# Attention stage of a four-layer kernel: the last pair of residual rows is loaded two steps later in the order, unused query columns hold ones, and whole output tiles are written

## The chip, the cores and the metric

The kernel runs on one core of a Trainium2 chip. The metric is the device time in microseconds (us); the median of the runs counts. The engines are PE (matrix multiply, with its weight load PEld), DVE (vector), ACT (scalar, activation functions), POOL (GpSimd) and SP, which here only issues DMAs. Each engine works through its own list of instructions in order; a DMA waits in its engine's list until its operands are ready, and what stands behind it in that list waits too.

## The reference

Four layers A, B, A, B with residuals, x of shape 1 x 2048 x 576:

```python
x = x + _A_ref(_layernorm(x), A_wqkv, A_wo)
x = x + _B_ref(_layernorm(x), B_w_in, B_w_sp, B_b_sp, B_w_out)
x = x + _A_ref(_layernorm(x), A_wqkv, A_wo)
x = x + _B_ref(_layernorm(x), B_w_in, B_w_sp, B_b_sp, B_w_out)
```

A is attention with 32 heads of 18 columns, in which each position looks at 8 keys: itself and the positions 2, 4, ... 14 before it. B is a gated layer: `z = gelu(x @ w_in)`, its second half is layer-normed and mixed over the sequence by a 2048 x 2048 matrix plus a bias, multiplied with the first half, and projected back by `w_out`.

## The kernel before

**Tiles of layer A.** The sequence is cut into 18 query tiles t of 114 rows (`QT`; tiles 8 and 17 have 112). A tile's keys are its own rows and the 14 before them, so 128 partitions of keys. Each tile is worked in two halves of 16 heads: steps s = 2t and 2t+1, 36 steps in all. In step s, PE computes the logits of step s+1 (`L_mm`, line 445), ACT takes the exponential into `P_sb` (`EXP`, line 454), PE multiplies the probabilities of step s with the values (`PV`, line 465; `v_ext` has a column of ones per head, so the sum of the probabilities comes out as a 19th column), and DVE divides: a reciprocal of those sums (`rec`, line 471) and a multiplication (line 472) into `o_t`. `P_sb` has 128 query columns, of which only 114 are computed; `setup_bufs` (lines 367 to 372) clears the others once, and clears the unused rows and columns of the three `o_t` buffers.

**From o_t to the residual.** After the second half of tile t, SP issues a DMA that transposes `o_t` into `o_slot` (line 475; called "transpose t" below). DVE copies the result into a ring `oT` (`O_CP`, line 484). The last two tiles are transposed on PE instead (`O_T`, line 490). When the ring holds 128 complete rows, PE projects row tile i with the output weights in two halves of the columns (`WO(i, 0)` and `WO(i, 1)`, line 510), and DVE adds the old x (`xo`) to give `x_new` (line 513). Then follow the statistics of the layer norm (DVE, lines 220 to 224, POOL line 225), the normalized rows (`LN_XN`, POOL lines 245 and 248, 2.3 us and 0.24 us), the store of `x_new` (`XST`, SP) and the transpose of the normalized rows into `xnT` for layer B (`LN_T`, SP, line 252). In layer 0 the normalized rows 4 to 12 are put into old staging buffers (`stg`).

**Residual loads.** `XO(i)` loads the old x of rows i and i+1 for even i in one DMA on SP, into one of two buffers `xo`. The buffer of pair 14 is that of pair 10, so the load must wait until `WO(11, 1)` has been added.

**Order.** All five engines follow one hand-made table: `at(s, f)` puts f into step s, after `PV(s)`, in the order in which `at` was called. With `row_step` as it is, both attention layers have `WO(11, 0)` in step 31, `WO(11, 1)` and `WO(12, 0)` in step 32, `WO(13, 0)` in step 34 and `WO(14, 0)` in step 35. `XO` is put five steps ahead of `WO`, so `XO(14)` stands in step 30 and `XO(12)` in step 27. Transpose 15 is issued by `PV(31)`, and its copy `O_CP(15)` stands in step 33.

**Layer B** follows without a break: in its first phase PE computes z (line 815), ACT applies gelu (line 829, into one of three buffers `zp`) and squares (line 833), DVE squares the rest (line 831) and normalizes (line 856), and POOL normalizes one block (line 858). POOL first issues the load of the bias (`b_sp`) into the memory that held the normalized rows of layer A; it waits until the last `LN_T` has read them. Then come phases in which PE is busy throughout (lines 905, 929, 971).

Of the kernel before, what the change touches and what calls it, by code (L numbers as in the profile page):

```python
# [10 lines left out]
ALU = mybir.AluOpType  # L11
# [7 lines left out]
P = 128  # L19
D = 576  # L20
H = 32
DH = 18
# [3 lines left out]
QT = P - HALO  # L26
# [39 lines left out]
class K:  # L66
# [258 lines left out]
    def layer_A(self, li):  # L325
        nc, tc, cfg = self.nc, self.tc, self.cfg
# [32 lines left out]
        def tdim(t):  # L359
            nq = cfg.tiles[t][1]  # L360
            return HALO + nq, nq
# [4 lines left out]

        def setup_bufs(eng):
            for pb in P_bufs:
                eng.memset(pb[:, :, :, QT:P], 0.0)
            for ob_ in o_bufs:  # L370
                eng.memset(ob_[96:P, :], 0.0)
                eng.memset(ob_[0:96, D:640], 0.0)

        def exp_table():
            nc.scalar.activation(out=P_bufs[0][:, 0, 0, 0:1], in_=self.ones[:, 0:1], func=ACT.Exp)
# [81 lines left out]
        def PV(s):  # L457
            t, hf = divmod(s, 2)
            nk, nq = tdim(t)
            O_ps = self.PT_tile([P, 512], f32, "O_ps")  # L460
            for jp in range(2):
                for ftl in range(4):
                    for jj in range(2):
                        idx = 4 * ftl + 2 * jp + jj
                        nc.tensor.matmul(O_ps[:, idx * (DH + 1):(idx + 1) * (DH + 1)],  # L465
                                         lhsT=P_bufs[(2 * s + jp) % 4][:nk, jj, ftl, :],
                                         rhs=v_ext[:nk, t, 16 * hf + idx, :], start=True, stop=True)
            Ov = O_ps[:, 0:16 * (DH + 1)].rearrange("p (h e) -> p h e", e=DH + 1)
            o_t = o_bufs[t % len(o_bufs)]
            rec = sb.tile([P, 16], f32, name="rec", tag="rec", bufs=2)  # L470
            nc.vector.reciprocal(out=rec[:nq, :], in_=Ov[:nq, :, DH])
            nc.vector.tensor_tensor(out=o_t[:nq, 288 * hf:288 * (hf + 1)].rearrange("p (h d) -> p h d", d=DH),
                                    in0=Ov[:nq, :, 0:DH], in1=rec[:nq, :, None].to_broadcast([nq, 16, DH]), op=ALU.mult)
            if hf == 1 and t < NT - 2:
                nc.sync.dma_start_transpose(out=o_slots[t % NSLOT][:], in_=o_t[:, :])

# [58 lines left out]
        if li == 0:  # L535
# [74 lines left out]
            R_(2, 2)  # L610
            rows[1]()
            setup_bufs(nc.gpsimd)
            rows[2](nc.gpsimd)
            A_(2, 3)
# [36 lines left out]
        else:  # L651
            for k_, (d, cc) in enumerate([(d, cc) for d in range(5) for cc in range(2)]):
                for qk in ((1, 0) if d < 4 else (0,)):
                    PG(d, qk, cc, k_ == 0, (nc.gpsimd, nc.sync, nc.gpsimd))
                if k_ == 0:
                    setup_bufs(nc.vector)
                    nc.vector.memset(v_ext[:, :, :, DH:DH + 1], 1.0)
                    self.fill_window_rows(QK, 0)
                    exp_table()
                if k_ == 1:  # L660
                    self.run_deferred()
                if k_ == 6:
                    self.fill_window_rows(QK, 1)
# [15 lines left out]
        def at(s, f, *a):  # L679
            table.setdefault(s, []).append((f, a))  # L680
# [12 lines left out]
        row_step = {}  # L693
# [5 lines left out]
                at(2 * t + (5 if li == 0 and t < 10 else 4), O_CP, t)  # L699
        for i in range(NS):  # L700
            s = row_step[i]
            at(s - 5, XO, i)
            at(s, WO, i, 0)
            at(s + 1, WO, i, 1)
            at(s + 1, LN_STATS, i)
            at(s + 2, LN_XN, i)
            at(s + 2, XST, i)
            if i < NS - 1:
                at(max(s + 4, 24 + (5 * i) // 4) if li == 0 else s + 4, LN_T, i)
# [21 lines left out]
        for s in range(NST):  # L731
            if s + 1 < NST:
                L_mm(s + 1)
                EXP(s + 1)
            PV(s)
            for f, a in table.pop(s, []):
                f(*a)
# [345 lines left out]
```

## Time and profile before

| | us |
|---|---|
| runs, median (lowest to highest of 3) | 1190.45 (1189.31 to 1191.66) |
| profiled execution, its own time | 1192.44 |
| span in its profile | 1190.6 |
| PE busy | 1167.5 (98%) |
| DVE busy | 554.3 (47%) |
| ACT busy | 376.9 (32%) |
| POOL busy | 285.9 (24%) |
| mean granted PE clock | 0.997 |

The profiled execution takes 1.84 us more than its span, and 1.99 us more than the median of the runs. In the profile "issue" is time in which an engine waited for nothing that is shown, SPq is SP's list of DMA issues, and `[0.5 <-X]` behind an instruction says that its engine stood idle 0.5 us before it and what ended that. Layer 0 (attention) lies at about 0 to 132 us, layer 1 at 132 to 598, layer 2 (attention) at 598 to 723, layer 3 at 723 to the end.

### The profile page before, as it was taken

What the parts mean: (1) busy time and instruction counts of PE and PEld (TensorE: products, weight loads), DVE (VectorE), ACT (ScalarE), POOL (GpSimd) and SP (SyncE); (2) the same over time, 40 slices, a digit from 0 to 9 for tenths busy, and PEclk for the clock granted to TensorE, in tenths of its full rate; (3) what the DMA queues carried; (4) which work ended last, traced back from release to release, by engine and by line L of the source; (5) the groups of instructions that cost most, each with busy time, mean ns of one, the idle gap of its engine ahead of it and who ended that gap; (6) DMA issues with size and microseconds to landing.
All of it is one profiled execution on the core that took longest, in us unless ns stands there. A gap on an engine that the chain in (4) does not pass through costs nothing.

```text
span 1190.6 us, 20417 instructions
## 1 busy us (share of the span) xinstructions
PE 1167.5 (98%) x8307; PEld 623.4 (52%) x8406; DVE 554.3 (47%) x1235; ACT 376.9 (32%) x621; POOL 285.9 (24%) x386
## 2 busy tenths in 40 slices
PE   9999999999999999999999989999999999999998
PEld 5567544444444444457755765444444444444676
DVE  8788676323233233235456875863223233232321
ACT  5578677111110111102156875770111110111000
POOL 4768774000000000002153876840000000000000
PEclk9999999999999999999999998999999999999999
DMA  7999993000000000059656997900000000001332
GB/s 190 200 173 203 188 220 58 23 12 12 12 1 12 12 12 1 18 169 275 159 94 128 207 211 168 231 10 14 12 12 12 12 1 12 12 1 35 117 105 73
DMA packets 179478, 101.57 MB, mean 85 GB/s; under 512 B 135711, under 2 KB 160735, under 8 KB 179384
## 3 DMA queue, kind: packets, MB, share of 16 engines
q1 hardware_dynamic: 166520, 78.50, 30.6%
q0 software_dynamic: 6512, 16.00, 5.4%
q10 hardware_dynamic: 6352, 5.75, 1.6%
q8 instruction: 66, 1.08, 0.4%
q14 instruction: 28, 0.23, 0.1%
HBM read 42.39 MB, written 16.53 MB: 49 GB/s over the span
## 4 chain that ended last, share of the span: by engine, by line
PE 89%; DMA 3%; POOL 3%; DVE 2%; issue 1%; ACT 1%; SPq 0%; ACTq 0%; POOLq 0%; DVEq 0%
PE pg L929 42%; PE po L971 12%; PE pz L815 10%; PE pz L905 6%; PE pz1s L905 6%; PE pp L410 4%; PE pw L510 2%; PE O_ps L465 2%; PE pv L387 2%; PE L_ps L445 2%; DMA o_slot<-o_t 2%; PE pzs L815 2%; POOL QK L80 1%; DMA xnT<-ln_xn 1%; ACT P_sb L454 1%
## 5 line engine op out<-in xcount | busy, mean ns | idle before, releaser
L929 PE MATMUL pg<-Wq,Z 128*128 128x512 bf16 x2258 | 497.8, 379 | 2.5
L929 PEld LDWEIGHTS <-Z 128*128 128x128 bf16 x2304 | 225.4, 98 | 271.8
L933 DVE TENSOR_TENSOR g_tmp<-pg,ln_xn 128x512 f32<-128x512 f32 x144 | 99.5, 691 | 422.3 <-PE pg L929 422.3
L924 ACT ACTIVATE z1T<-pz 128x1024 bf16<-128x1024 f32 x36 | 34.9, 1020 | 497.4 <-PE pz L905 493.8
L80 POOL DMA_DIRECT2D wout<-in_B_w_out_dram x4 | 4.3, 1064 | 600.8 <-PE pg L929 600.8
L971 PE MATMUL po<-wout,Z 128*128 128x288 bf16 x1152 | 141.4, 286 | 0.0
L454 ACT ACTIVATE P_sb<-L_ps 128x912 bf16<-128x912 f32 (+1 forms) x144 | 125.8, 929 | 39.9 <-PE L_ps L445 39.1
L971 PEld LDWEIGHTS <-Z 128*128 128x128 bf16 x1152 | 112.7, 98 | 28.8
L815 PEld LDWEIGHTS <-xnT 128*128 128x128 bf16 (+1 forms) x800 | 66.5, 97 | 83.7 <-issue 26.5
L815 PE MATMUL pz<-win2a,xnT 128*128 128x512 bf16 x380 | 103.9, 380 | 2.4 <-ACT zp L829 1.6
L934 DVE TENSOR_TENSOR Z<-g_tmp,z1T 128x512 bf16<-128x512 f32 x144 | 99.7, 692 | 12.9 <-DVE g_tmp L933 0.9
L905 PEld LDWEIGHTS <-w 128*128 128x128 bf16 (+1 forms) x640 | 53.7, 97 | 74.0 <-issue 13.6
L410 PE MATMUL pp<-xnT,wqk_sb 128*128 128x512 bf16 x341 | 81.4, 379 | 2.2 <-DMA xnT<-ln_xn 0.9
L829 ACT ACTIVATE zp<-pz 128x1024 bf16<-128x1024 f32 x64 | 65.4, 1022 | 35.4 <-PE pz L815 16.9
L981 DVE TENSOR_TENSOR x_new<-po,xo 128x288 f32<-128x288 f32 (+1 forms) x64 | 28.8, 455 | 87.8 <-PE po L971 84.3
L905 PE MATMUL pz<-xnT,w 128*128 128x512 bf16 (+1 forms) x314 | 66.2, 380 | 0.3
L905 PE MATMUL pz1s<-xnT,w 128*128 128x512 bf16 (+1 forms) x312 | 65.3, 379 | 0.7 <-issue 0.6
L831 DVE CUSTOM_DVE_ANT_0 Z<-zp 128x1536 bf16<-128x1536 bf16 x32 | 56.5, 1765 | 15.6 <-ACT zp L829 10.0
L815 PE MATMUL pz<-win2b,xnT 64*128 64x512 bf16 (+1 forms) x240 | 59.7, 380 | 0.0
L80 POOL DMA_DIRECT2D QK<-stg x81 | 50.6, 630 | 36.7 <-DVE stg L379 18.5
L245 POOL TENSOR_SCALAR ln_xn<-x_new,ln_mv,ln_rstd 128x576 bf16<-128x576 f32 x23 | 54.4, 2367 | 2.0
L510 PE MATMUL pw<-wo_sb,oT 128*128 128x288 bf16 x320 | 50.7, 296 | 3.8 <-DVE oT L484 3.7
(120 smaller groups left out, 1008.3 us busy)
## 6 DMA issues: line engine op xcount, KB each, us to landing
xres<-x_new SPq DMA_DIRECT2D x48, 288.0 KB
xo<-xres SPq DMA_DIRECT2D x32, 288.0 KB
wout<-in_B_w_out_dram POOLq DMA_DIRECT2D x4, 1296.0 KB, 8.3
xo<-xres SPq DMA_DIRECT2D x8, 576.0 KB
w<-in_B_w_in_dram SPq DMA_DIRECT2D x16, 256.0 KB
QK<-stg POOLq DMA_DIRECT2D x53, 72.0 KB, 4.6
QK<-stg SPq DMA_DIRECT2D x41, 72.0 KB
xo<-in_A_x_dram SPq DMA_DIRECT2D x8, 288.0 KB
```

What stands on the lines that cost most here:

```text
L80: return eng.dma_start(out=out, in_=in_)
L410: nc.tensor.matmul(pp[:, :], lhsT=w, rhs=self.xnT[:, c, PADL + cc * 512:PADL + (cc + 1) * 512], start=(c == 0), stop=(c == 4))
L454: nc.scalar.activation(out=P_bufs[(2 * s + jp) % 4][:nk, :, :, 0:nq], in_=Lv[:nk, :, :, 0:nq], func=ACT.Exp, scale=scale)
L510: nc.tensor.matmul(pw[:, 0:288], lhsT=oT[:, c, r0:r0 + P], rhs=wo_sb[:, c, hh * 288:(hh + 1) * 288], start=(c == 0), stop=(c == 4))
L815: nc.tensor.matmul(pzvs[ci][:, sub * 512:sub * 512 + w], lhsT=self.xnT[r0:r1, c, PADL + i * P:PADL + (i + 1) * P], rhs=win2(c)[r0:r1, c0 + ...
L829: nc.scalar.activation(out=zp[:, c0:c0 + cn], in_=pzvs[ci][:, 0:cn], func=ACT.Gelu_apprx_tanh, accum_out=sums[:, ci:ci + 1])
L831: nc.vector.tensor_tensor_reduce(out=spare[:, 0:SQ_D], in0=zp[:, 0:SQ_D], in1=zp[:, 0:SQ_D], scale=1.0, scalar=0.0, op0=ALU.mult, op1=ALU. ...
L905: nc.tensor.matmul(outs[a_], lhsT=w1[r0:r1, c, sub * P:(sub + 1) * P], rhs=self.xnT[r0:r1, c, PADL + q * 512:PADL + (q + 1) * 512], start= ...
L929: nc.tensor.matmul(pg[:, :], lhsT=Z[:, jj, i, sub * P:(sub + 1) * P], rhs=Wq[q][:, i, :], start=(i == 0), stop=(i == NS - 1))
L933: nc.vector.tensor_tensor(out=tmp[:], in0=pg[:, :], in1=bsp[:, qs], op=ALU.add)
L934: nc.vector.tensor_tensor(out=uT(jj)[:, sub, qs], in0=tmp[:], in1=z1Ts[jj, sub][:, qs], op=ALU.mult)
L971: nc.tensor.matmul(acc[hh], lhsT=uT(j // 2)[:, j % 2, i * P:(i + 1) * P], rhs=wouts[j // NJH][:, j % NJH, hh * 288:(hh + 1) * 288], start= ...
```

## The change

```diff
         def setup_bufs(eng):
             for pb in P_bufs:
-                eng.memset(pb[:, :, :, QT:P], 0.0)
+                eng.memset(pb[:, :, :, QT:P], 1.0)
             for ob_ in o_bufs:
-                eng.memset(ob_[96:P, :], 0.0)
-                eng.memset(ob_[0:96, D:640], 0.0)
+                eng.memset(ob_[:, D:640], 0.0)
...
-            nc.vector.reciprocal(out=rec[:nq, :], in_=Ov[:nq, :, DH])
-            nc.vector.tensor_tensor(out=o_t[:nq, 288 * hf:288 * (hf + 1)].rearrange("p (h d) -> p h d", d=DH),
-                                    in0=Ov[:nq, :, 0:DH], in1=rec[:nq, :, None].to_broadcast([nq, 16, DH]), op=ALU.mult)
+            nc.vector.reciprocal(out=rec[:], in_=Ov[:, :, DH])
+            nc.vector.tensor_tensor(out=o_t[:, 288 * hf:288 * (hf + 1)].rearrange("p (h d) -> p h d", d=DH),
+                                    in0=Ov[:, :, 0:DH], in1=rec[:, :, None].to_broadcast([P, 16, DH]), op=ALU.mult)
...
         for i in range(NS):
             s = row_step[i]
-            at(s - 5, XO, i)
+            if i % 2 == 0:
+                at(max(s - 5, row_step[i - 3] + 1) if i >= 4 else s - 5, XO, i)
             at(s, WO, i, 0)
             at(s + 1, WO, i, 1)
```

With ones in the unused query columns, the sums of the unused output rows are positive numbers, so that all 128 rows can be divided and written, and `o_t` needs clearing only in columns 576 to 639. `setup_bufs` runs on POOL in layer 0 and on DVE in layer 2; in both its six `o_t` memsets (three of 32 x 640 and three of 96 x 64) become three of 128 x 64, and its four `P_sb` memsets stay. In layer 2 these four wrote 128 x 56 words of 32 bits each before and write 128 x 112 bf16 values now. Lines from 372 to 700 move up by one number.

`XO` for odd i did nothing before, so leaving it out changes nothing. `XO(12)` goes from step 27 to 28, with no other SP instruction between. `XO(14)` goes from step 30 to 32. The lists of SP's instructions differ in this one place per attention layer. In layer 0 the order was XO(14), transpose 15, LN_T, XST(10), LN_T; it is now transpose 15, LN_T, XST(10), LN_T, XO(14). In layer 2 it was XO(14), transpose 15, LN_T(9), XST(10); it is now transpose 15, LN_T(9), XST(10), XO(14). PE's and ACT's lists keep their order, DVE's and POOL's lose the three memsets each. PE's `O_T` no longer waits for POOL's clearing.

## The prediction

> **What bounds the kernel now.** I read the engines' shares on the page first, then the chain of waits, then the timelines at the two ends of attention.
>
> ```profile
> PE 1167.5 (98%) x8307; PEld 623.4 (52%) x8406; DVE 554.3 (47%) x1235; ACT 376.9 (32%) x621; POOL 285.9 (24%) x386
> ```
>
> PE is busy 98% and holds 89% of the chain, so a change off PE can only win PE's few gaps, or matmuls that ran at a lower clock. The largest gap that touches the edited code lies at the end of layer 2. The chain there:
>
> ```profile
> 708.31 0.02 SPq L80
> 708.33 0.05 issue
> 708.38 5.78 DMA o_slot<-o_t
> 714.16 0.02 issue
> 714.18 0.35 DVE oT L484
> 714.53 0.05 issue
> 714.58 1.38 PE pw L510 x5
> ```
>
> PE waits for O_CP(15), that for transpose 15, and that for an SP instruction of line 80. SP's timeline says which:
>
> ```profile
> 703.26 0.57 SPq L80 DMA_DIRECT2D xres<-x_new  x1
> 707.96 0.37 SPq L80 DMA_DIRECT2D xo<-xres  x1
> 708.38 1.20 SPq L475 DMA_TRANSPOSE o_slot<-o_t  x1
> ```
>
> SP stands from 703.83 to 707.96 at XO(14), whose buffer is still read. The DVE and PE rows show who has waited for what:
>
> ```profile
> 705.00 0.46 DVE L472 TENSOR_TENSOR o_t<-O_ps,rec 114x288 bf16<-114x288 f32 x1
> 707.49 0.45 DVE L513 TENSOR_TENSOR x_new<-pw,xo 128x288 f32<-128x288 f32 x1
> 711.67 0.15 DVE L224 TENSOR_SCALAR ln_rstd<-ln_mv 128x1 f32<-128x1 f32 x1
> 714.18 0.34 DVE L484 COPY oT<-o_slot 128x570 bf16<-128x570 bf16 x1 [2.36 <-DMA o_slot<-o_t]
> 714.58 1.38 PE L510 MATMUL pw<-wo_sb,oT 128*128 128x288 bf16 x5 [3.04 <-DVE oT L484]
> ```
>
> Tile 15 was complete at 705.46; WO(11, 1) freed the xo buffer at 707.94. DVE had nothing to do from 711.82 to 714.18, PE from 711.54 to 714.58. The gap costs twice, as three stretches of 1 us show (first the stretch and its length, then each engine's busy time; the third number from the right is PE's granted clock, 1.00 in full):
>
> ```profile
> 714.00:715.00 1.00, 0.42 (x2) 0.28 (x3) 0.78 (x3) 0.00 (x0) 1.00 (x1) 0.50 1.07 352
> 719.00:720.00 1.00, 1.00 (x6) 0.60 (x4) 0.86 (x4) 0.00 (x0) 0.14 (x1) 0.50 0.60 235
> 721.00:722.00 1.00, 0.93 (x7) 0.49 (x6) 0.89 (x3) 0.98 (x2) 1.00 (x1) 1.00 0.20 76
> ```
>
> The clock is 1.00 up to 713, falls in the microsecond from there, and is 0.50 until about 720.5. Layer 0 runs the same instructions at full clock: there the same group of five starts at 126.52 after 0.62 us idle, and the last WO ends at 132.17, 5.65 us later. Layer 2 needs 714.58 to 722.93, 8.35 us. So the low clock costs 2.7 us.
>
> **Part 1, XO(14) in layer 2.** Transpose 15 can be issued at about 705.5 in place of 708.38. It took 5.78 us behind the 576 KB load; transpose 14 took 5.23. Landing at 710.7 to 711.3 is ahead of 711.82, when DVE comes to O_CP(15), so DVE's own list is late next: 2.36 us are won and 0.68 of PE's 3.04 us remain, like layer 0's 0.62, which kept the clock. PE's end of attention is then 712.22 + 5.65 = 717.87, 5.05 us earlier. Not all of that lasts. POOL's chain of normalized rows is next: it starts row 13 at 719.87 before; in layer 0 it starts 3.90 us after PE's group of five (130.42 against 126.52), so at 716.12 now, 3.75 us earlier. At about 3.2 us a row it then runs back to back to row 15, whose LN_T frees the memory for the bias load; behind that load stands the first normalized block (line 858), which frees the first zp. Before, ACT already waited for that, 1.29 us at 738.89, and PE's fifth row began at 740.06 with no room left. So PE gives back 1.3 us near 736, and 3.7 us remain. Bounds: 2.4 (DVE's wait alone, clock or POOL give nothing) and 5.05 (POOL is not late).
>
> **What the moved load costs.** XO(14) issues behind LN_T(9) (rows ready since 703.34), and XST(10). Their issue takes 1.2, 1.3 and 0.6 us: XO(14) at about 708.75, 0.8 later than before. Row 14 needs it at 719.73 before, at 716.0 now (layer 0: 3.77 after the group of five). Cover 7.2 us; transpose 15, issued right behind it and waiting in the same list, landed 6.2 us after XO(14) was issued. I cost it at nothing; without cover every us late is a us of DVE's addition.
>
> **Part 2, XO(14) in layer 0.** SP was free at 121.25 and issued XO(14) at 121.87; tile 15's rows had been there since 119.37. SP then issues without a pause until 137.67, ending with LN_T(12) and XST(15), and these end the wait of ACT's line 833 at 139.74, after which PE has 1.58 us idle at 141.73. SP's list is what is late, so its stall less one issue gap (0.62 - 0.1), 0.5 us, is won; bounds 0.3 (DVE's wait at O_CP(15) alone) and 0.7. XO(14) itself now issues behind transpose 15, two LN_T and XST(10) at 126.0, and row 14's addition comes at 130.29 - 0.3. Four us of cover against 3.83 for transpose 15 here and 5.78 in layer 2: up to 1.8 us late. That is hidden by POOL, which starts row 14 at 133.63, 1.3 us after its statistics: I cost it at 0, with 0.5 as the bad end.
>
> **Part 3, setup.** In layer 0 POOL's list holds up DVE:
>
> ```profile
> 11.87 0.63 POOL L371 MEMSET o_t<- 32x640 bf16 x1
> 12.54 0.15 POOL L372 MEMSET o_t<- 96x64 bf16 x1
> 15.26 0.73 POOL L576 TENSOR_TENSOR lnx_rstd<-lnx_rstd,neg_half 128x2 f32<-128x2 f32 x1
> 16.03 0.77 DVE L583 TENSOR_SCALAR ln_xn<-x_in,lnx_mv,lnx_rstd 128x576 bf16<-128x576 bf16 x2 [2.27 <-POOL lnx_rstd L576]
> 23.31 10.95 PE L410 MATMUL pp<-xnT,wqk_sb 128*128 128x512 bf16 x49 [0.40 <-DMA xnT<-ln_xn]
> ```
>
> Six memsets take 11.87 to 14.46; three of 128 x 64 at 0.15 take 0.45, so POOL and DVE win 2.1 us. PE is busy from 12.89 to 22.91 with other work and waits only 0.40 us for these rows, then 0.52 at 52.12 for later ones. I take 0.6; bounds 0 (transfers fill the time: their share is about 1 up to 16 us and again from 44) and 0.92. In layer 2 the six take 1.6 us of DVE's time, but DVE then stands idle 1.96 us ahead of 605.25 for another reason: 0. The four P_sb memsets in their new form cost at most POOL's 0.19 us each for the same size, against 0.105: 0.34 us, inside the same idle time.
>
> **Part 4, 128 rows instead of 114.** 72 reciprocals and 72 multiplications. The rows of 112 and 114 partitions take 0.24, 0.25 and 0.46, 0.46; the addition on 128 x 288 takes 0.45. Partitions cost nothing; 0. If time grew with them (12% of 0.71 us, 72 times) DVE would lose 6.1 us, partly beside PE; the rows exclude it. PE's PV already writes all 128 rows, so nothing is added there.
>
> **Sum.** 3.7 + 0.5 + 0.6 = 4.8 us. The profiled execution of 1192.44 (span 1190.6 and 1.84 around it) would become 1187.6; the median of the runs is 1.99 lower and becomes 1190.45 - 4.8 = 1185.65, say 1185.6.
>
> **A rule against it.** The row: PE last worked at 711.54 before the gap, and the clock fell between 713 and 714. The Trainium skill, "TensorE: Matmul & The Clock Gate", Part 1, has the clock halve after an idle window of about 3.4 us that runs freely; by that page a gap of 3.04 us need not halve it in every run, and the sum would then be 3.5 us, the first rival. The trace has it after a shorter gap, so I take the trace.
>
> **Rivals.** *The clock is not won:* it stays low after 712, or the unprofiled runs of before did not lose it. For it: a gap of 0.68 remains behind one of 0.42. Against: layer 0 has 0.41 and 0.62 at clock 1.00. Layer 2 then gives 2.4, the sum 3.5: 1187.0. *The transpose does not land earlier:* it is issued earlier but queues behind LN_T(8) and XST(9), so layer 2 gives nothing. For: transfers at a share above 1 from 695 to 705. Against: the share is 0.00 at 707 to 708, the queue has run dry. Then 1.1 remain: 1189.4. *Slower, the late residual load:* XO(14) takes longer in its new place than its cover. At 4 us late in each layer (loads of 8 and 11 us) it takes 2.7 us in layer 0 beyond POOL's 1.3 of slack, and in layer 2 4 us plus 2.7 as the clock drops in the new gap, 9.4 against the 4.8 won: 1195.0. It turns the sign by more than the noise from about 3 us late in each. For: transfers are near their full share there. Against: the 6.2 us above.
>
> **How the numbers follow.** Forecast 0.60, clock 0.16, no earlier landing 0.15, slower 0.09. A measurement of this kernel can tell about 0.2%, 2.4 us, from no change: below 1188.1 is faster. The forecast and most of the clock case lie there (0.75); the third case and the rest are the same (0.16). The forecast's own bounds are 2.7 to 6.7 us won, 1183.8 to 1187.8; with 1.1 us for the median of three runs, and towards the third case, the range is 1182.8 to 1189.2.
>
> **What would show it.** Right: SP issues transpose 15 right after tile 15 is complete, PE's 3.04 us wait shrinks to about 0.7, no stretch at clock 0.50 there, a new PE wait for ACT of about 1.3 us in the first rows of layer 3, POOL's first memset group 2.1 us shorter. Wrong: DVE's x_new waits for the xo load, transpose 15 still lands near the end of DVE's wait, or a stretch at clock 0.50 remains.

## The result, and the profile after

| | us |
|---|---|
| changed kernel, median (lowest to highest of 13 runs) | 1187.38 (1184.22 to 1189.9) |
| kernel before beside it, median (lowest to highest of 13 runs) | 1193.82 (1189.31 to 1197.04) |
| ratio, with its 95% interval | 0.9947 [0.9933, 0.996] |
| profiled execution of the changed kernel, and its span | 1188.89, 1187.1 |

The ratio is 6.3 us off 1193.82 (4.8 to 8.0). The kernel before ran higher here than in the three runs shown ahead of the prediction (1190.45); in all sets below its median lies between 1192.6 and 1195.4, and that of the changed kernel between 1186.8 and 1187.4. The two profiled executions differ by only 3.5 us in their spans: the one of after lost time in layer 0, as the rows at the end of this section show, and two further executions of the same kernel (below) lost less or nothing there.

The engines' line of the page after has three DVE and three POOL instructions fewer and 1.2 us less PE time. Its clock was low for 6.8 us in before and for 3.4 us in after (in layer 0, from 75.6 us):

```profile
PE 1166.3 (98%) x8307; PEld 622.3 (52%) x8406; DVE 554.9 (47%) x1232; ACT 377.3 (32%) x621; POOL 287.6 (24%) x383
```

SP's timeline at the end of layer 2 (start, duration, instruction). Transpose 15 is issued 0.6 us after tile 15 was complete at 706.16, and the residual load stands three places behind it, without a wait:

```profile
706.79 1.24 SPq L474 DMA_TRANSPOSE o_slot<-o_t  x1
708.13 1.22 SPq L252 DMA_TRANSPOSE xnT<-ln_xn  x1
709.40 0.57 SPq L80 DMA_DIRECT2D xres<-x_new  x1
710.07 0.38 SPq L80 DMA_DIRECT2D xo<-xres  x1
```

The timelines of DVE and PE there. DVE goes from the statistics straight into O_CP(15) at 712.51, so the transpose had landed; PE's idle time before WO(13, 0) is 0.48 us in place of 3.04. In the last row, in layer 3, PE waits for ACT's gelu. That had begun at 735.46, right after POOL's first normalized block (its row stands with POOL's below: 733.48 and 1.95 us); the profile puts ACT's wait down to a DVE instruction of line 842, which ended at the same 735.43:

```profile
712.44 0.15 DVE L224 TENSOR_SCALAR ln_rstd<-ln_mv 128x1 f32<-128x1 f32 x1
712.51 0.60 DVE L483 COPY oT<-o_slot 128x570 bf16<-128x570 bf16 x1
712.30 0.38 PE L815 MATMUL pz<-win2a,xnT 128*128 128x512 bf16 x1 [0.42 <-ACT P_sb L453]
713.16 0.79 PE L509 MATMUL pw<-wo_sb,oT 128*128 128x288 bf16 x5 [0.48 <-DVE oT L483]
736.63 0.81 PE L815 MATMUL pz<-win2a,xnT 128*128 128x512 bf16 x3 [0.55 <-ACT zp L829]
```

Stretches of 1 us (PE's clock is the third number from the right): it is 1.00 in every one, and the last WO ends 5.65 us after WO(13, 0) started, in place of 8.35:

```profile
713.00:714.00 1.00, 0.84 (x10) 0.72 (x11) 0.73 (x4) 0.06 (x1) 0.90 (x3) 1.00 1.38 326
714.00:715.00 1.00, 1.00 (x26) 0.90 (x23) 0.78 (x3) 0.70 (x2) 1.00 (x1) 1.00 0.88 124
719.00:720.00 1.00, 1.00 (x8) 0.32 (x7) 1.00 (x3) 0.37 (x1) 1.00 (x1) 1.00 0.98 380
```

POOL's timeline: the `o_t` clearing takes 0.33 us instead of 2.6, the next reciprocal root comes at 12.80 (before 15.26), row 13 of layer 2 starts 3.90 us after WO(13, 0), and the bias load (before at 734.67) ends POOL's chain, with the first normalized block behind it:

```profile
11.64 0.33 POOL L371 MEMSET o_t<- 128x64 bf16 x3
12.80 0.72 POOL L575 TENSOR_TENSOR lnx_rstd<-lnx_rstd,neg_half 128x2 f32<-128x2 f32 x1
717.06 0.56 POOL L225 TENSOR_TENSOR ln_rstd<-ln_rstd,neg_half 128x1 f32<-128x1 f32 x1 [0.62 <-DVE ln_rstd L224]
731.23 0.64 POOL L80 DMA_DIRECT2D ln_xn<-in_B_b_sp_dram  x1 [3.25 <-issue]
733.48 1.95 POOL L858 TENSOR_SCALAR Z<-zp,z_rstd,z_nmr 128x256 bf16<-128x256 bf16 x1
```

PE in layer 0. Before, PE stood 1.09 us at 37.80 for `v_ext` (the values) and 0.52 at 52.12. The row of before:

```profile
37.80 2.61 PE L387 MATMUL pv<-wv_sb,xnT 128*128 128x288 bf16 x20 [1.09 <-DVE v_ext L379]
```

In after the first wait is gone, the second is 0.25, and PE stands 1.74 us ahead at 50.38. Then it waits 2.45 us for the copy of transposed tile 2, where before it had no wait there, and starts WO(13, 0) 2.35 us behind, at 128.87:

```profile
33.77 5.17 PE L386 MATMUL pv<-wv_sb,xnT 128*128 128x288 bf16 x40
50.38 1.24 PE L409 MATMUL pp<-xnT,wqk_sb 128*128 128x512 bf16 x4 [0.25 <-DMA xnT<-ln_xn]
73.58 0.79 PE L509 MATMUL pw<-wo_sb,oT 128*128 128x288 bf16 x5 [2.45 <-DVE oT L483]
143.38 0.81 PE L815 MATMUL pz<-win2a,xnT 128*128 128x512 bf16 x3 [0.88 <-ACT zp L829]
```

### The profile page after: what moved, and what is told of

It is laid out like the page before. It is cut to its first block, busy times and chain, and to the rows that moved or that the text cites. A ratio compares the mean times of both kernels' runs of the same rounds, so it can differ in the third digit from the quotient of the medians.

```text
span 1187.1 us, 20409 instructions
## 1 busy us (share of the span) xinstructions
PE 1166.3 (98%) x8307; PEld 622.3 (52%) x8406; DVE 554.9 (47%) x1232; ACT 377.3 (32%) x621; POOL 287.6 (24%) x383
## 5 line engine op out<-in xcount | busy, mean ns | idle before, releaser
L386 PE MATMUL pv<-wv_sb,xnT 128*128 128x288 bf16 (+1 forms) x360 | 52.8, 286 | 0.6 <-DVE o_t L471 0.5
```

## Experiments

Twelve kernels ran in three sets of four, each set on one chip beside the kernel before. Lines added or left out shift the line numbers of a kernel by a few. "Won" is one minus the ratio, times the median of before in that set. The difference of the two medians is another reading of the same runs, and the two can be 2 us apart: down the table it is 3.9, 2.1, 2.1, -0.5, then 8.6, 8.3, 6.9, 2.5, then 4.5, 4.3, 2.5, 5.4.

| kernel | median us (runs) | before | ratio [95%] | won, us |
|---|---|---|---|---|
| xo_only | 1189.81 (9) | 1193.68 | 0.9963 [0.9944, 0.9983] | 4.4 |
| setup_only | 1191.58 (12) | 1193.68 | 0.9976 [0.9959, 0.9992] | 2.9 |
| xo_layer2 | 1191.54 (12) | 1193.68 | 0.9963 [0.9945, 0.9981] | 4.4 |
| xo_layer0 | 1194.21 (12) | 1193.68 | 0.9992 [0.9975, 1.0008] | 1.0 |
| after_again | 1186.83 (6) | 1195.39 | 0.993 [0.9911, 0.9948] | 8.4 |
| pool_back | 1187.05 (6) | 1195.39 | 0.9939 [0.9917, 0.9961] | 7.3 |
| xo_late | 1188.53 (8) | 1195.39 | 0.9947 [0.9925, 0.9969] | 6.3 |
| fill_gap | 1192.94 (12) | 1195.39 | 0.9977 [0.9961, 0.9992] | 2.7 |
| win_late | 1188.09 (12) | 1192.58 | 0.9971 [0.995, 0.9991] | 3.5 |
| win_mid | 1188.33 (12) | 1192.58 | 0.9972 [0.9957, 0.9987] | 3.3 |
| xo_only_again | 1190.13 (12) | 1192.58 | 0.9977 [0.9961, 0.9993] | 2.7 |
| after_third | 1187.17 (5) | 1192.58 | 0.996 [0.9948, 0.9972] | 4.8 |

An interval is some 2 us wide to each side, so the runs alone cannot place a term of half a microsecond. The traces can, if the same stretch is measured in each. This table has four such stretches of each profiled execution: when WO(13, 0) starts in layer 0; the time from PE's first matmul of layer 3 (line 815, just ahead of WO(13, 0) in layer 2) to its first group of the large product (line 905); inside that, from the start of that first matmul to WO(13, 0); and from WO(13, 0) to the end of the last WO, which is 5.65 at full clock.

| kernel | WO(13, 0), layer 0 | 815 to 905 | to WO(13, 0) | WO(13, 0) to last WO |
|---|---|---|---|---|
| *XO(14) of layer 2 in its old place* | | | | |
| before | 126.52 | 84.58 | 3.42 | 8.35 |
| setup_only | 130.52 | 83.01 | 3.10 | 7.13 |
| xo_layer0 | 132.22 | 84.11 | 3.55 | 7.78 |
| *XO(14) of layer 2 moved* | | | | |
| after | 128.87 | 80.00 | 0.86 | 5.65 |
| after_again | 125.90 | 80.43 | 1.29 | 5.65 |
| after_third | 124.88 | 79.99 | 0.85 | 5.65 |
| xo_only | 127.81 | 79.99 | 0.85 | 5.65 |
| xo_only_again | 127.43 | 81.89 | 1.29 | 7.12 |
| xo_layer2 | 126.68 | 80.72 | 1.30 | 5.64 |
| pool_back | 126.60 | 80.21 | 1.09 | 5.65 |
| xo_late | 127.72 | 80.42 | 1.29 | 5.65 |

Means of the column "815 to 905": 83.90 in the old place, 80.46 in the new: 3.4 us won. It is 3.5 with the old setup (84.35 to 80.87) and 2.8 with the new (83.01, one execution, to 80.21). `win_late` and `win_mid`, changed kernels that follow below, have 80.43 and 80.00. The first column runs from 124.88 to 132.22, 7.3 us apart, and both groups scatter.

The clock can be read in every run, since each has its span and its mean granted clock on record. One minus the clock, times the span, is the time that the low clock takes from a PE that is always busy. It is 4.4 us on the mean of the 80 runs of before in these three sets, against 2.1 on the mean of the 71 runs of the eight kernels with the load of layer 2 moved (each to within 0.4 us); `setup_only` has 4.3, `xo_layer0` 4.7 and `xo_layer2` 2.2 (each to within about 1). So some 2.3 us of low clock went with the move of that load, over all runs and not only in the profiled ones.

**The two parts apart.** `xo_only` takes only the move of `XO`:

```diff
-            at(s - 5, XO, i)
+            if i % 2 == 0:
+                at(max(s - 5, row_step[i - 3] + 1) if i >= 4 else s - 5, XO, i)
```

> The kernel before with the XO edit alone (both attention layers). Theory 1 (the late load held up transpose 15, and the edit wins the wait and PE's clock at the end of layer 2): 4 to 5.5 us faster than before, PE's wait for O_CP(15) in layer 2 about 0.5 us instead of 3.04, no microsecond at clock 0.50 there. Theory 2 (the cheaper setup carries half of the measured 6.4 us): 2 to 3.5 us faster.

It won 4.4 us (2.0 to 6.7), which covers both theories; its trace is that of theory 1, with the stretches of after at the end of layer 2, 0.47 us of wait before WO(13, 0) and no low clock there. `setup_only` takes the rest of the change (ones, three short memsets, 128 rows) and leaves `XO` where it was. Its diff is that of the change without this piece:

```diff
-            if i % 2 == 0:
-                at(max(s - 5, row_step[i - 3] + 1) if i >= 4 else s - 5, XO, i)
+            at(s - 5, XO, i)
```

> The kernel before with the ones, the 128-row division and the smaller clearing, but XO as before. Theory 1: within 1 us of before; PE is about 1.5 us ahead at 40 us of layer 0 (its wait of 1.09 us near 37 is gone) and loses it again at a wait for a transpose of o_t near 72; layer 2 keeps the 3 us wait and the clock 0.50. Theory 2: 2 to 3.5 us faster.

It won 2.9 us (1.0 to 4.9), more than the 0.6 of my sum and in the range of theory 2. The two together are 7.3, against 6.3, 8.4 and 4.8 for the whole in three sets, so they add up within the noise. One reading of theory 1 missed: PE's wait for `v_ext` is still there, and PE is not ahead. POOL's list was 2.2 us earlier, as meant (its reciprocal root at 13.01 in place of 15.26), but DVE then waited 2.71 us, until 18.42, for a load of x that landed late; that wait is 0.89 us in after, 0.23 in `after_again`, and not in before:

```profile
38.43 2.61 PE L386 MATMUL pv<-wv_sb,xnT 128*128 128x288 bf16 x20 [0.93 <-DVE v_ext L378]
```

In its trace the wait in layer 2 has stayed, and the clock falls, but later and for a shorter time than in before (PE's row, then the stretches):

```profile
718.07 0.79 PE L509 MATMUL pw<-wo_sb,oT 128*128 128x288 bf16 x5 [2.73 <-DVE oT L483]
```

```profile
718.00:719.00 1.00, 0.93 (x11) 0.81 (x12) 0.73 (x4) 0.00 (x0) 0.94 (x2) 0.97 1.19 341
719.00:720.00 1.00, 1.00 (x22) 0.82 (x19) 0.71 (x3) 0.69 (x2) 0.08 (x1) 0.50 1.03 406
722.00:723.00 1.00, 1.00 (x11) 0.82 (x10) 0.87 (x4) 0.00 (x0) 0.42 (x1) 0.82 0.79 295
```

A microsecond at mean clock c was at half clock for 2(1 - c) of it. Here that is 0.06 + 3 + 0.36 = 3.42 us; in before (0.87 at 713, 0.50 to 720, 0.72 at 720) 0.26 + 6 + 0.56 = 6.82 us. PE was already working when the clock fell at 718.94.

**One layer at a time.** `xo_layer2` is `xo_only` with one more condition, and `xo_layer0` has `li == 0` in its place:

```diff
-                at(max(s - 5, row_step[i - 3] + 1) if i >= 4 else s - 5, XO, i)
+                at(max(s - 5, row_step[i - 3] + 1) if i >= 4 and li > 0 else s - 5, XO, i)
```

> The kernel before with the XO edit in layer 2 alone. Theory 1: 3.7 to 4.8 us faster, nearly all of the XO edit. Rival (layer 0's saturated SP list is the larger part): under 2 us.

> The kernel before with the XO edit in layer 0 alone. Theory 1: 0.3 to 0.7 us faster, not clear of the noise, and the wait and the clock 0.50 stay in layer 2. Rival: 2 us or more faster.

`xo_layer2` won as much as `xo_only` by ratios (4.4; by medians 2.1 against 3.9), and its stretch to line 905 is as short: the gain lies in layer 2. Its PE rows are those of after, with a slightly longer give-back:

```profile
710.47 0.79 PE L510 MATMUL pw<-wo_sb,oT 128*128 128x288 bf16 x5 [0.92 <-DVE oT L484]
734.21 0.81 PE L816 MATMUL pz<-win2a,xnT 128*128 128x512 bf16 x3 [0.84 <-ACT zp L830]
```

`xo_layer0` is not told apart from before (1.0 us, -1.0 to 3.0). From PE's first line 815 to line 905, layers 0 and 1 take 79.8 to 81.2 us with the load of layer 0 in its old place (four executions: 81.16, 80.15, 79.80, 80.26, mean 80.3) and 79.3 to 81.0 with it moved (eight, mean 80.0): 0.3 us in a scatter of 1.7. Its trace also shows the wait for transposed tile 2, longer than in after, in a kernel whose setup is that of before, and the old wait and half clock in layer 2:

```profile
76.18 0.79 PE L510 MATMUL pw<-wo_sb,oT 128*128 128x288 bf16 x5 [3.64 <-DVE oT L484]
720.80 1.38 PE L510 MATMUL pw<-wo_sb,oT 128*128 128x288 bf16 x5 [3.18 <-DVE oT L484]
```

**Is the wait in layer 0 a cost of the change?** The changed kernel once more, as it is:

> The changed kernel once more, as the reference of this set and for a second profile of it. Both theories expect the median of its runs within 1.5 us of 1187.4. They differ on PE's new wait of 2.45 us for the copy of transposed tile 2 at 73.6 us in layer 0. Theory 1 (scatter): the landing time of that transpose differs from execution to execution, so the wait of this profile differs from 2.45 us by more than 0.7 us or stands at another tile. Theory 2 (a cost of the change): the earlier start pushes the transpose behind the loads, so the wait is there again, at the same tile, with 2.0 to 2.9 us.

The wait came again at tile 2 with 1.03 us in place of 2.45, and in `after_third` it was not there at all. So theory 1: the landing of that transpose scatters, and the 2.35 us lost in layer 0 in the first profile belong to that execution and not to the change.

```profile
72.26 0.79 PE L509 MATMUL pw<-wo_sb,oT 128*128 128x288 bf16 x5 [1.03 <-DVE oT L483]
```

**What POOL's clearing is worth.** The changed kernel with the long clearing given back to POOL in layer 0 alone:

```diff
             for ob_ in o_bufs:
-                eng.memset(ob_[:, D:640], 0.0)
+                if li == 0:
+                    eng.memset(ob_[96:P, :], 0.0)
+                    eng.memset(ob_[0:96, D:640], 0.0)
+                else:
+                    eng.memset(ob_[:, D:640], 0.0)
```

> The changed kernel, but POOL clears the old six o_t regions again in layer 0 (2.6 us in place of 0.3 to 0.5 us of its list); layer 2 and the rest stay changed. Theory 1 (chain of POOL, DVE, window rows, POOL's transfers and normalized rows): POOL's and DVE's rows of 13 to 36 us stand 1.4 to 2.4 us later than in the changed kernel, PE waits about 1.1 us for v_ext near 37.8 us again, and PE's projections after it stand 1.2 to 1.8 us later at 52 us; the time is 1.2 to 2.9 us above that of the changed kernel. Theory 2 (my prediction's term): PE waits only where it did before, 0.4 and 0.5 us, so 0.6 us above (0 to 0.9). Theory 3 (the gain of the part that has the setup alone came from layer 2 or from scatter): no difference beyond 0.3 us.

POOL's rows move as theory 1 said, by 2.4 us (12.78 in `after_again`, 15.17 here), and PE's wait for `v_ext` is back:

```profile
15.17 0.73 POOL L579 TENSOR_TENSOR lnx_rstd<-lnx_rstd,neg_half 128x2 f32<-128x2 f32 x1
38.19 2.61 PE L390 MATMUL pv<-wv_sb,xnT 128*128 128x288 bf16 x20 [0.99 <-DVE v_ext L382]
```

But WO(13, 0) of layer 0 starts at 126.60, 0.70 us after that of `after_again` and between those of the other two executions of the changed kernel, and the time is 0.2 us above by medians and 1.1 by ratios. So the longer chain of theory 1 exists in PE's waits. What it is worth at the end is not shown: `after_again` stood again at 48.12 (0.70 us) and 72.26 (1.03) behind transfers, and the runs, 0.2 to 1.1 us with intervals of over 2 us, leave room for all three theories.

**The late residual load.** The changed kernel, with `XO(14)` only one step ahead of `WO(14, 0)`:

```diff
-                at(max(s - 5, row_step[i - 3] + 1) if i >= 4 else s - 5, XO, i)
+                at(s - 1 if i == 14 else max(s - 5, row_step[i - 3] + 1) if i >= 4 else s - 5, XO, i)
```

> The changed kernel, but the last pair of residual rows is loaded two steps later still (one step ahead of its use; in layer 2 behind one more transpose and two stores, issue about 713.6 us instead of 710.1; in layer 0 about 132 instead of 128.8). Theory 1 (the cover of the load is real and short): the load takes 3.5 to 6 us, so DVE waits 0.5 to 3 us for it at row 14 in each layer; POOL's own backlog hides about 1.3 us of each; 0.5 to 4 us above the changed kernel, most likely 2. Theory 2 (the load has slack left): it lands in under 3 us, DVE waits for it nowhere, and the time is within 0.8 us of the changed kernel's.

SP's rows of the two issues, then DVE's additions of row 14 that wait for them:

```profile
129.43 0.42 SPq L80 DMA_DIRECT2D xo<-in_A_x_dram  x1
711.24 0.44 SPq L80 DMA_DIRECT2D xo<-xres  x1
```

```profile
132.71 0.82 DVE L512 TENSOR_TENSOR x_new<-pw,xo 128x288 f32<-128x288 f32 x2 [1.17 <-DMA xo<-in_A_x_dram]
715.89 0.82 DVE L512 TENSOR_TENSOR x_new<-pw,xo 128x288 f32<-128x288 f32 x2 [0.43 <-DMA xo<-xres]
```

The load takes 3.3 us in layer 0 and 4.6 in layer 2 from issue to use. In the changed kernel it has 3.83 us in layer 0 (128.80 to row 14 at 132.63) and 6.86 in layer 2 (710.07 to 716.93), so in layer 0 only half a microsecond is left over, and DVE's only wait for a residual row in the attention layers is 0.46 us, at 67 us for an early pair. With the cover gone DVE waits 1.17 and 0.43 us; PE waits 0.46 us for that once in layer 0, and the stretches to line 905 are as long as in the changed kernel (79.87 and 80.42), since POOL is behind in any case. By ratios it is 2.0 us above `after_again`, but the two intervals overlap. Theory 1 holds for the mechanism; what it does to the time the runs do not tell.

**The clock by itself.** The kernel before, with 46 small matmuls on the identity put into PE's gap in layer 2:

```diff
+        def FILL():
+            fl = self.PT_tile([P, 512], f32, "fill")
+            for _ in range(46):
+                nc.tensor.matmul(fl[:, 0:P], lhsT=self.ident[:], rhs=self.ident[:], start=True, stop=True)
+        if li > 0:
+            at(34, FILL)
         for i in range(NS):
```

> The kernel before, but in layer 2 PE runs 46 small extra matmuls on the identity (some 2.5 us, results unused) in step 34 just ahead of the group of WO(13, 0), that is inside the gap of 3.04 us; the residual load and the setup stay as before, so the wait itself stays. Theory 1 (the gap costs twice): PE still stands until about 714.5 us for the copy of transposed tile 15, but every stretch behind it has the clock at 1.00 and the last WO of layer 2 ends 5.6 to 5.9 us after that group's start instead of 8.35; POOL's rows gain only about 1.4 us of it, so 1.3 to 2.7 us below the kernel before, 2.0 most likely. Theory 2 (the clock's fall costs nothing in the end, since POOL's rows or DVE set the first phase of layer 3): within 0.7 us of the kernel before. Theory 3 (the extra matmuls themselves run late and hold up WO): 0 to 2 us above it.

PE's rows: the fill lies in the gap, 1.51 us of it remain, and the wait for O_CP(15) stays. The stretch behind it is at full clock:

```profile
715.10 2.73 PE L703 MATMUL fill<-ident 128*128 128x128 bf16 x46
719.34 0.79 PE L510 MATMUL pw<-wo_sb,oT 128*128 128x288 bf16 x5 [1.51 <-DVE oT L484]
743.37 0.81 PE L821 MATMUL pz<-win2a,xnT 128*128 128x512 bf16 x3 [0.70 <-ACT zp L835]
```

```profile
719.00:720.00 1.00, 0.67 (x6) 0.55 (x7) 0.89 (x3) 0.00 (x0) 1.00 (x1) 1.00 1.09 340
```

The last WO ends 5.64 us after WO(13, 0), so the low clock is gone; from there to line 905 PE needs 74.07 us against 72.8 in the three executions of the old order: 1.3 us given back where it waits for ACT's `zp`. Of 2.1 us (mean of 2.70, 1.48 and 2.13) 0.8 would remain; the runs say 2.7 (1.0 to 4.7), and their low clock takes 2.2 us in place of 4.4. So the half clock costs time by itself. That the wait costs more besides rests on the traces (0.8 us here, 3.4 with the load moved); the intervals of the runs overlap.

**The transfers of layer 0.** The changed kernel with the six loads of win2a in steps 13 to 18 (`win_late`), or with 8 in place of 13 in steps 8 to 13 (`win_mid`), instead of step 0:

```diff
-            for f in reversed(self.load_win2a(nc.gpsimd)):
-                at(0, f)
+            for k_, f in enumerate(reversed(self.load_win2a(nc.gpsimd))):
+                at(13 + k_, f)
```

> The changed kernel, but in layer 0 POOL issues the six loads of win2a (288 KB each, needed only near 125 us) one a step in steps 13 to 18 instead of all in step 0 (44 to 50 us), where in every trace the transfers are at their full share and the transposed rows or tile 2 land 1 to 4 us late by turns. Theory 1 (these loads are what the transposes collide with): the group of WO(13, 0) in layer 0 starts at 125.0 to 126.5 us, and the median is 1 to 3 us below the changed kernel's. Theory 2 (the transfers of window rows fill the time by themselves): within 0.8 us. Theory 3 (the loads now stand in POOL's list between normalized rows, 0.65 us each, and crowd the late transposes): 1 to 3 us above.

> As the kernel above, with the six loads in steps 8 to 13 (about 70 to 82 us). Theory 1: like it, 0.5 to 3 us below the changed kernel, since the crowded stretch of 44 to 62 us loses 1.7 MB. Theory 2: within 0.8 us. Theory 3 (the stretch of 64 to 75 us is just as crowded, and the first normalized rows of POOL wait): 0.5 to 2 us above.

Neither shows a gain: 0.9 and 1.2 us above `after_third` by medians, 1.3 and 1.4 by ratios, inside the intervals. The collision moves. PE's waits for transposed tiles in `win_late` come at 100 and 110 us instead of 73, and cost the clock as well (1.38 us for five matmuls instead of 0.79):

```profile
99.92 1.38 PE L509 MATMUL pw<-wo_sb,oT 128*128 128x288 bf16 x5 [2.25 <-DVE oT L483]
110.00 1.38 PE L509 MATMUL pw<-wo_sb,oT 128*128 128x288 bf16 x5 [2.26 <-DVE oT L483]
```

**The setup part once more**, as `xo_only` beside the changed kernel on one chip:

> Only the residual load is moved, setup and 128 rows as before; run beside the changed kernel on the same chip, to see what the setup part is worth. Theory 1 (long chain through POOL, DVE and the window rows): 1.2 to 2.9 us above the changed kernel. Theory 2 (my term of 0.6): 0 to 0.9 above. In the profile both expect layer 2 as in the first run of it: from the first projection of layer 2 to the first group of the large product of layer 3 (line 905 in the kernel before) 192.8 to 194.0 us, against 197.2 to 198.0 where the load stands in its old place.

> The changed kernel for comparison in this set. Median within 1.5 us of 1187.0; layer 2 and the start of layer 3 (same two marks) 192.8 to 194.0 us; the group of WO(13, 0) in layer 0 anywhere from 125.9 to 130 us.

The changed kernel is 3.0 us below `xo_only_again` by medians and 2.0 by ratios; in the first sets 1.9 by ratios. With the 2.9 of `setup_only` the setup part is worth 2 to 3 us, each comparison with some 2 us to either side. Three readings missed. WO(13, 0) in layer 0 of `after_third` starts at 124.88. From the first projection of layer 2 to line 905 `after_third` needs 194.30 us and `xo_only_again` 197.38, as long as in the old order, because its clock fell twice there: from 690.11, and again from 714.00 though it has the short gap of the moved load:

```profile
712.40 0.59 PE L816 MATMUL pz<-win2a,xnT 128*128 128x512 bf16 x2 [0.42 <-ACT P_sb L454]
713.69 1.12 PE L510 MATMUL pw<-wo_sb,oT 128*128 128x288 bf16 x5 [0.70 <-DVE oT L484]
```

```profile
713.00:714.00 1.00, 0.31 (x3) 0.26 (x4) 0.97 (x4) 0.16 (x1) 0.94 (x3) 1.00 2.25 214
714.00:715.00 1.00, 1.00 (x9) 0.74 (x8) 0.43 (x2) 0.00 (x0) 0.90 (x2) 0.50 0.22 22
717.00:718.00 1.00, 1.00 (x8) 0.73 (x7) 1.00 (x3) 0.00 (x0) 0.00 (x0) 0.79 0.51 112
```

Half clock from 714.00 for 3.4 us costs 1.47 us there (7.12 against 5.65).

## Why the prediction was right or wrong

The sign, the place and the mechanism were right, and the time lies in the range. The forecast of 1185.6 us was 1.8 below the 1187.38 measured: the gain was 1.6 larger than my 4.8, and the base of 1190.45 was 3.4 lower than the median of before over 13 runs. The two misses partly cancelled, which is luck.

- **Layer 2 (3.7 us).** Right: 3.4 us by the traces of eight executions against three, 2.7 to 4.4 by the runs of three kernels. The mechanism held, but that the size came out so close is partly luck: two of its terms were off and cancelled. The wait in front of WO(13, 0): 2.36 forecast, 2.26 measured (3.36 to 1.10, means of the third stretch). The clock: 2.7 forecast, 2.70, 1.48 and 2.13 in the three executions of the old order, and 1.47 of it not won in one of eight of the new: 1.9 on the mean (2.3 by the clock of all runs). The give-back near 736: 1.3 forecast, 0.7 measured (from the last WO to line 905: 72.8 before, 73.5 after). I let POOL's chain move by the start of row 13 alone. Counted from the first line 815, that start moved 3.95 us (8.71 to 4.76), but the bias load that ends the chain moved 4.58 (23.51 to 18.93), because in before the normalization of row 15 took 3.86 us instead of 2.29, where in after a row was stretched by 1.2, and the bias load followed 3.55 us behind that row, where in after it took 3.25. One row stretched by 1.1 to 1.6 us stands in all fourteen traces; what stretches it is open.
- **The rule on the clock.** The low stretches of layer 2 measure 3.42 us (`setup_only`, `xo_only_again`) or 6.82 us (before, `xo_layer0`: 0.22 + 6 + 0.60). The Trainium skill, "TensorE: Matmul & The Clock Gate", Part 1, gives the gate a free-running window of 3413 ns. One and two such windows are what the runs show, and a free phase fits a cost that was not the same in every execution. That it takes an idle window to halve the clock is not what the runs show: in `xo_only_again` PE had idled 1.12 us (0.42 and 0.70) of the 3.42 before the fall. My sum took the one trace's 2.7 as fixed.
- **Layer 0's end (0.5 us).** Not shown and not refuted: 1.0 (-1.0 to 3.0) by the runs, 0.3 by the traces.
- **Setup (0.6 us).** The one term that failed: 2 to 3 us by the runs. I listed PE's gaps at 23.31 and 52.12 as all that the chain from POOL's clearing could win and left out the 1.09 us for `v_ext` at 37.80, which has the same source (POOL, DVE's filling of the window rows, POOL's transfers of `QK`, the last four normalized rows). I also took POOL's list as the only thing that DVE waits for there; in `setup_only` a late load of x took its place (2.71 us), and the `v_ext` wait stayed. Giving the clearing back to POOL (`pool_back`) cost 0.2 to 1.1 us by the runs, which their intervals do not tell from nothing. What the rest is stays open: layer 2's memsets, the ones, the 128 rows or scatter. No stretch of the traces shows it. The clock of the runs leaves room for a part: it takes 1.6 us on the mean of the 24 runs of the changed kernel and 2.4 in the 33 with the load moved alone, each to within 0.6, but in `setup_only` it takes as much as in before. An execution's layer 0 varies by 7.3 us, too much to find it there.
- **128 rows (0).** Right: the reciprocal takes 0.25 and the multiplication 0.46 us on 128 rows, as on 114.
- **XO(14)'s new place (0).** Right: there is no wait for it, and its load (3.3 and 4.6 us) stays below the cover (3.83 and 6.86), so the slower rival had no ground, in layer 0 by half a microsecond only. The rival without an earlier landing fell with PE's 0.48 us; the rival without the clock came true in one of eight profiled executions, but not on the mean of the runs.

## What to carry to other kernels

Ahead of a DMA that must wait for a buffer, look at what stands behind it in its queue: moving the waiting load behind the instructions that are ready cost nothing that the traces show, as the load took less time than its new cover. Cost a gap on PE twice, by the wait and by the clock behind it, and take the second as a spread over the executions, not as one figure. Before a short trace difference is read as gain or loss, measure the same stretch in several executions: here a stage that the change hardly touches moved by more than the whole gain.

## What the runs showed of the hardware

- PE's clock fell sixteen times in the fourteen profiled executions (the falls at their ends left out), twelve times for 3.41 us and four times for 6.83, never for another length. All times between two changes of one execution are whole multiples of 3.413 us (20.48 and 634.88 in `xo_only_again`, 6 and 186 times). It fell 2.2 us after PE's last work in before, 0.9 us after PE had resumed in `setup_only`, and with 1.12 us of idle time in the 3.41 us ahead of it in `xo_only_again`; gaps of 1.12 and 1.34 us in `after_again` and `xo_layer2`, and one of 1.51 in `fill_gap`, did not bring it down.
- With transfers at a share of 1.0 to 1.3, a DMA transpose of 128 x 640 took 8.8 us from issue to use (tile 2 in layer 0 of after, 64.42 to 73.19); in layer 2 transpose 15, issued at 706.79, had landed before 712.51. The start of layer 0's last group moved from 124.88 to 132.22 us between executions with it, and taking 1.7 MB of other loads out of that stretch did not end it.
- Clearing by POOL follows the elements per partition: 0.63 us for 32 x 640, 0.15 us for 96 x 64, 0.33 us for three of 128 x 64.
